# Sparse attention and a feed-forward layer on one core: the third batch's first transposes go ahead of a load, and four units of matmuls move in front of its scores

## The chip, the core and the metric

The kernel runs on one core of a Trainium2 chip. The core has a matrix engine (TensorE, PE in the profile), a vector engine (VectorE, DVE), a scalar engine (ScalarE, ACT) that applies functions and copies, a general engine (GpSimd, POOL) and a queue that gives out transfers (SyncE, SP). All work side by side, and each takes its own instructions in order: what waits at the head of an engine's queue holds whatever stands behind it. The metric is device time of the whole program in microseconds (us), as the median of several executions.

## The reference

Eight batches of eight heads, head size 64. Each head has 512 local and 32 global positions. A local query sees its neighbours up to 32 away and all global keys; a global query sees everything. The outputs of all heads are put side by side and go through a feed-forward layer with a hard-swish.

```python
s_g = scale * q_g @ concat(k_g, k_l).T           # global rows see everything
out_g = softmax(s_g) @ concat(v_g, v_l)
s_ll = where(abs(i - j) <= 32, scale * q_l @ k_l.T, -1e9)
s_l = concat(scale * q_l @ k_g.T, s_ll)
out_l = softmax(s_l) @ concat(v_g, v_l)
x = concat(out_g, out_l) -> (8 * 544, 512)       # heads side by side
h = x @ w_in                                     # 512 -> 2048
g = h * clip(h + 3, 0, 6) / 6
out = g @ w_out                                  # 2048 -> 512
```

## The kernel before

**Attention** works on pairs of heads. A batch has four pairs (NM is 4), so the program has 32 pairs, numbered p = 4 * batch + m. For each pair:

- `load(p)` gives SP the transfers of k, q and v into staging buffers (`stg`, 16 of them, 256 KB each); a transfer can be given only when its buffer is free.
- `cast(p, "kq", nc.gpsimd)` has POOL turn them into 16-bit `kn` and `qn`. `first(p, what)` casts and also copies half of v to other partitions (`vshift`).
- k and q must be transposed. For the first two batches TensorE does this (`emit_T`). From the third batch on (pair 8 = `2 * NM`) `emit_TD(p)` gives SP two DMA transposes, L244 for k into `kT`, L245 for q into `qT`.
- `wrap_q(p)` (L251) has ScalarE copy the last 32 columns of the transposed q to its front. It waits for the q transpose.
- `emit_S2(p)` multiplies the scores (L263, 16 small matmuls into four PSUM buffers), takes their exponentials on ScalarE (L267) and masks them on VectorE (L270). Pair p's scores read what `wrap_q(p)` wrote.
- `emit_SG(p)` does the global queries' scores, `emit_AV(p)` multiplies by v and normalises, `emit_PG(p)` does the global rows' sums, and `emit_X(p)` transposes the result for the feed-forward layer.

**The feed-forward layer** is cut into units that `M(n)` places between the steps of attention, n at a time, from a list. A unit `u1(c)` is four matmuls (L421) into one PSUM buffer, an evicting function on ScalarE (L426, writes `t`) and a product on VectorE (L428, writes `gt`). A unit `u2(t, c4)` is four matmuls (L437) of the second product; every fourth one is copied out and stored (L441, L443). The pool `psp` has seven PSUM buffers, shared by scores, units and transposes. A batch's units come into the list after its attention, so they run beside the next batch.

**The order.** Up to `wrap_q(2 * NM)` and the unit behind it, all five engines' orders are fixed as the program is written, by `pin(*ALL)`. From there on only the transfer queue and POOL are fixed (`pin(*QUEUES)`); the order on TensorE, VectorE and ScalarE is chosen when the program is built, by a scheduler, and it may put a later instruction ahead of the fixed ones where its operands allow.

Around the third batch's start the program is written like this (the parts that the change touches):

```python
    emit_TD(2 * NM)                # transposes of pair 8
    load(2 * NM + 2)               # pair 10
    ...
    emit_TD(2 * NM + 1)            # transposes of pair 9
    ...
    M(4)
    emit_den(1)                    # global rows of batch 1: a matmul,
    emit_XG(1)                     # logarithms (L405), an exponential (L406)
    wrap_q(2 * NM)
    M(1)
    pin(*ALL)
    emit_S2(2 * NM)
```

In the loop that follows, `feed(p)` calls `wrap_q(p + 1)`, casts pair p + 4, gives the transposes of pair p + 3 and the loads of pair p + 5; then come the scores of pair p + 1, the attention of pair p, and units in four groups n[0] to n[3] between them.

Of the kernel before, what the change touches and what calls it, by code (L numbers as in the profile page):

```python
# [14 lines left out]
def kernel(  # L15
# [12 lines left out]
    nc = tc.nc  # L28
# [5 lines left out]
    NM = H // 2  # L34
# [20 lines left out]
    def ps_tile(name, dtype=FP32):  # L55
        return psp.tile([P, 2048 // (4 if dtype == FP32 else 2)], dtype, tag="ps", name=name)
# [54 lines left out]
    def stage():  # L111
        return wrk.tile([P, 512], FP32, tag="stg", name="stg", bufs=NSTG)

    def load(p, what="kqv"):
        b, m = divmod(p, NM)
        s = st.setdefault(p, {})
        for c in what:
            src = {"k": k_l, "q": q_l, "v": v_l}[c]
            t = stage()
            if c != "v" and b < NRUN:  # L120
                nc.sync.dma_start(out=t.rearrange("p (h x) -> p h x", h=2),  # L121
                                  in_=src[b, 2 * m:2 * m + 2].rearrange("h (p j) d -> p h (j d)", j=NT))
            else:
                nc.sync.dma_start(out=t.rearrange("p (h kb d) -> p (h kb) d", h=2, kb=NT),
                                  in_=src[b, 2 * m:2 * m + 2].rearrange("h (kb p) d -> p (h kb) d", p=P))
            s[c + "f"] = t.rearrange("p (h kb d) -> p kb h d", h=2, kb=NT)

    def cast(p, what, eng):
        b, m = divmod(p, NM)
        s = st[p]  # L130
        for c in what:
            if c == "v":
                o = vts[b % NV][:, :, m, vc].rearrange("p kb (h d) -> p kb h d", h=2)
            else:
                s[c + "n"] = wrk.tile([P, NT, P], FP16, tag=c + "n", name=c + "n", bufs=4)
                o = s[c + "n"].rearrange("p kb (h d) -> p kb h d", h=2)
            eng.tensor_copy(out=o, in_=s[c + "f"])  # L137
# [27 lines left out]
    def cast_w(kind, i, eng):  # L165
        if kind == "in":
            qd, m = divmod(i, NM)
            o = w_in_t[m][:, qd * 512:(qd + 1) * 512]
        else:
            o = w_out_t[i // 4][:, i % 4]  # L170
        (eng.copy if eng is nc.scalar else eng.tensor_copy)(out=o, in_=w_st[kind, i])  # L171
# [13 lines left out]
    def cast_G(b0, b1, nm, eng=nc.vector):  # L185
        n = wrk.tile([P, 4 * P], FP16, tag="gn", name=nm + "n", bufs=2)
        nb = b1 - b0
        eng.tensor_copy(out=n[:, 0:nb * P], in_=gst[b0, nm][:, 0:nb * P])
        gst[b0, nm, "n"] = n
# [23 lines left out]
    def emit_T(p, qdve=False):  # L213
        b, m = divmod(p, NM)
        s = st[p]
        kT = kTs[b % 2][:, m]
        kv = kT[:, 0:NT * KW].rearrange("p (u c) -> p u c", u=NT)
        qT = wrk.tile([P, Sl + W], FP16, tag="qT", name="qT", bufs=5)
        ps = {}
        for c in "kq":  # L220
            ps[c] = ps_tile("psT" + c, FP16)[:, 0:Sl]
            for j in range(NT):
                nc.tensor.matmul(out=ps[c][:, j * P:(j + 1) * P], lhsT=s[c + "n"][:, j], rhs=ident,
                                 is_transpose=True)
        qcopy = nc.vector.tensor_copy if qdve else nc.scalar.copy
        nc.vector.tensor_copy(
            out=kv[:, :, 0:P].rearrange("p u (i j) -> p u i j", j=NT),
            in_=ps["k"].rearrange("p (j u i) -> p u i j", j=NT, u=NT))
        qcopy(out=qT[:, W:Sl + W].rearrange("p (i j) -> p i j", j=NT),
              in_=ps["q"].rearrange("p (j i) -> p i j", j=NT))  # L230
        if b == 0:
            nc.vector.tensor_copy(out=qT[:, 0:W], in_=qT[:, Sl:Sl + W])
        else:
            nc.scalar.copy(out=qT[:, 0:W].rearrange("p (i j) -> p i j", j=NT),
                           in_=ps["q"].rearrange("p (j i) -> p i j", j=NT)[:, P - W // NT:P])
        s["qT"], s["kT"] = qT, kT

    def emit_TD(p):
        b, m = divmod(p, NM)
        s = st[p]  # L240
        kT = kTs[b % 2][:, m]
        kv = kT[:, 0:NT * KW].rearrange("p (u c) -> p u c", u=NT)
        qT = wrk.tile([P, Sl + W], FP16, tag="qT", name="qT", bufs=5)
        nc.sync.dma_start_transpose(out=kv[:, :, 0:P], in_=s["kn"].rearrange("p u c -> p (u c)"))  # L244
        nc.sync.dma_start_transpose(out=qT[:, W:Sl + W].rearrange("p (u c) -> p u c", u=NT),  # L245
                                    in_=s["qn"].rearrange("p u c -> p (u c)"))
        s["qT"], s["kT"] = qT, kT

    def wrap_q(p):
        qT = st[p]["qT"]  # L250
        nc.scalar.copy(out=qT[:, 0:W], in_=qT[:, Sl:Sl + W])  # L251
# [130 lines left out]
    def emit_X(p):  # L382
        b, m = divmod(p, NM)
        xn = st[p]["xn"]
        if b > 3 or (b == 3 and m < NM - 1):
            xt = wrk.tile([P, Sl], FP16, tag=f"xt{m}", name=f"xt{m}", bufs=2)
            xts.setdefault(b, []).append(xt)
            nc.sync.dma_start_transpose(out=xt.rearrange("p (w c) -> p w c", w=NT),
                                        in_=xn.rearrange("p w c -> p (w c)"))
            return  # L390
        psX = ps_tile("psX", FP16)
        for w in range(NT):
            nc.tensor.matmul(out=psX[:, w * P:(w + 1) * P], lhsT=xn[:, w], rhs=ident,
                             is_transpose=True)
        xt = wrk.tile([P, Sl], FP16, tag=f"xt{m}", name=f"xt{m}", bufs=2)
        xts.setdefault(b, []).append(xt)
        nc.vector.tensor_copy(out=xt, in_=psX[:, 0:Sl])

    def emit_XG(b):
        pg = pgs[b]  # L400
        Lg = wrk.tile([P, NM, Sg], FP32, tag="Lg", name="Lg", bufs=1)
        Rg = wrk.tile([P, NM, Sg], FP32, tag="Rg", name="Rg", bufs=1)
        for e in range(2):
            r = slice(e * D, (e + 1) * D)
            nc.scalar.activation(out=Lg[r], in_=pg[r, 1, :, e], func=LN)  # L405
        nc.scalar.activation(out=Rg, in_=Lg, func=EXP, scale=-1.0)  # L406
        for e in range(2):
            r = slice(e * D, (e + 1) * D)
            nc.vector.tensor_tensor(out=xg[r, :, b], in0=Rg[r], in1=pg[r, 0, :, e], op=mult)
# [56 lines left out]
    def M(n):  # L466
        for _ in range(n):
            if units:
                units.pop(0)()

    def local_dests(b):
        d = []
        for t in range(NT):
            row = b * S + Sg
            if t == 0:
                d.append([(W, P - W, row), (0, W, row + Sl - W)])
            else:
                d.append([(0, P, row + t * P - W)])
        return d
# [28 lines left out]
    for i in range(8, NC):  # L508
        load_w("out", i)
    load(2 * NM, "v")  # L510
    load(2 * NM + 1)

    wz = const("wz", [P, P])
    nc.vector.memset(wz, 0.0)
# [80 lines left out]
    cast(2 * NM, "kq", nc.gpsimd)  # L595
    for i in range(8, NC):
        cast_w("out", i, nc.gpsimd)
    cast(2 * NM + 1, "kq", nc.gpsimd)
    units += moe_units(lambda mm: xts[0][mm], Sl, local_dests(0), early=True)
    u1 = units.pop(0)  # L600
    emit_T(0)
# [34 lines left out]
        u1(c, range(3, 4))  # L636
    u1(4)
    u1(5)
    emit_T(4)
    cast_G(1, 4, "kg")  # L640
    u1(6)
    emit_T(5)
    emit_G(1, 4, "kg")
    emit_S(4, 0)
# [31 lines left out]
    emit_SG(1)  # L676
    M(1)
    emit_TD(2 * NM)
    load(2 * NM + 2)
    emit_X(7)  # L680
    sum_E(0)
# [68 lines left out]
    M(4)  # L750
    emit_den(1)
    emit_XG(1)
    wrap_q(2 * NM)
    M(1)
    pin(*ALL)
# [5 lines left out]
    for p in range(2 * NM, NPAIR):  # L761
        b, m = divmod(p, NM)
        feed(p)
        if p == 10:
            load_g(4, B, "kg")
            load_g(4, B, "qg")
        if p == 12:
            cast_G(4, B, "kg", nc.gpsimd)
            cast_G(4, B, "qg", nc.gpsimd)
        if p == 14:  # L770
            emit_G(4, B, "kg")
        n = (1, 1, 1, 2) if p == 2 * NM else (1, 2, 2, 2) if b in (3, 4) else (1, 2, 2, 3)
        M(n[0])
        if m == 0 and b > NRUN:
            emit_den(b - 1)
            emit_XG(b - 1)
        if p + 1 < NPAIR:
            emit_S2(p + 1)
        M(n[1])
        if p + 1 < NPAIR:  # L780
            emit_SG(p + 1)
        M(n[2])
        emit_AV(p)
        emit_PG(p)
        M(n[3])
        if p == 14:
            emit_G(4, B, "qg")
        emit_X(p)
        if m == NM - 1:
            units += moe_units(lambda mm, b=b: xts[b][mm], Sl, local_dests(b), last=(b == B - 1))  # L790
        pin(*QUEUES)
# [41 lines left out]
```

## Time and profile before

| what | value |
|---|---|
| median of 7 runs | 330.67 us (328.84 to 331.51) |
| the profiled execution's own time | 330.65 us |
| its span on the core | 328.8 us |
| TensorE busy | 308.1 us (94%) |
| VectorE, ScalarE, POOL busy | 217.6, 200.6, 153.1 us |
| mean granted TensorE clock | 0.99 |
| longest wait of TensorE | 7.46 us, before the scores of pair 8 |

The views are read like this. A row of a timeline is start, duration, engine, source line, operation, tiles out and in, shapes, how many instructions were merged, and in brackets the idle time before it with what ended it. A row of the waits is engine, line and what it waited for, then total us, number, longest. A row of the windows is a stretch with each engine's busy time and instruction count in the order PE, PE weight loads, DVE, ACT, POOL, then the granted clock, the DMA engines' busy share and GB/s. SP's rows show the time in which its queue was occupied with an issue; when a transfer lands is told apart from that.

### The profile page before, as it was taken

How to read it: one execution, taken by the hardware profiler on the slowest of the kernel's cores; microseconds unless marked ns; L12 is line 12 of the kernel's file. 1: busy time of each engine (PE TensorE's matmuls, PEld its weight loads, DVE VectorE, ACT ScalarE, POOL GpSimd, SP SyncE). 2: the span in 40 equal slices, each digit the busy share in tenths (PEclk: the TensorE clock that was granted, in tenths of full speed). 3: DMA queues.
4: the chain of work that ended last, by engine and by line, in shares of the span. 5: the costliest groups of instructions: out<-in, count | busy, mean ns of one | idle time of the engine just before them, and what ended most of it. 6: DMA issues, size and time to landing. Idle time of an engine off the chain costs nothing.

```text
span 328.8 us, 7315 instructions
## 1 busy us (share of the span) xinstructions
PE 308.1 (94%) x2673; PEld 163.1 (50%) x2673; DVE 217.6 (66%) x485; ACT 200.6 (61%) x420; POOL 153.1 (47%) x270
## 2 busy tenths in 40 slices
PE   7898999909899999999999989999999999999995
PEld 5553555505455545554455545554555554448444
DVE  6758687828745499857886679458945882379201
ACT  6768877639434499438855777558845971379100
POOL 4877797686944753685447644743521110000000
PEclk9999999978999999999999999999999999999999
DMA  8999999999889978888789978898833102100131
GB/s 214 255 299 313 249 280 308 186 223 204 147 195 230 207 140 146 180 201 175 145 148 214 201 150 146 200 190 158 149 100 107 33 16 77 68 0 3 32 98 64
DMA packets 140260, 53.05 MB, mean 161 GB/s; under 512 B 127552, under 2 KB 131904, under 8 KB 140224
## 3 DMA queue, kind: packets, MB, share of 16 engines
q1 hardware_dynamic: 138048, 52.32, 70.3%
q0 software_dynamic: 2176, 0.26, 1.3%
q8 instruction: 21, 0.34, 0.5%
q14 instruction: 15, 0.12, 0.1%
HBM read 35.13 MB, written 8.91 MB: 134 GB/s over the span
## 4 chain that ended last, share of the span: by engine, by line
PE 57%; DMA 16%; DVE 7%; ACT 6%; POOL 6%; issue 4%; SPq 3%; POOLq 0%; ACTq 0%
PE po L437 29%; PE psH L421 18%; DMA stg<-in_v_l_dram 4%; DVE gt L428 3%; ACT t L426 3%; DMA stg<-in_moe_w_out_dram 3%; DMA qT<-qn 3%; PE psS L263 2%; DMA stg<-in_moe_w_in_dram 2%; DMA stg<-in_q_l_dram 2%; POOL vt L137 2%; SPq L121 2%; ACT E L267 2%; DMA stg<-in_k_l_dram 1%; DVE E L270 1%
## 5 line engine op out<-in xcount | busy, mean ns | idle before, releaser
L437 PE MATMUL po<-wout,gt 128*128 128x512 f16 x528 | 122.8, 379 | 0.3 <-POOL wout L171 0.3
L421 PE MATMUL psH<-xt,win 128*128 128x512 f16 x512 | 121.1, 381 | 2.0 <-DVE gt L428 1.4
L428 DVE SCALAR_TENSOR_TENSOR gt<-t,psH 128x512 f16<-128x512 f32 (+1 forms) x144 | 90.0, 652 | 41.6 <-ACT t L426 40.7
L426 ACT ACTIVATE t<-psH,half_col 128x512 f32<-128x512 f32 (+1 forms) x144 | 91.1, 671 | 12.4 <-PE psH L421 11.2
L421 PEld LDWEIGHTS <-win 128*128 128x128 f16 x576 | 53.5, 98 | 53.2 <-issue 3.5
L437 PEld LDWEIGHTS <-gt 128*128 128x128 f16 x528 | 48.5, 98 | 52.7 <-DVE kgT L206 0.4
L270 DVE TENSOR_TENSOR E<-E,mk 128x512 f16<-128x512 f16 x96 | 54.1, 605 | 7.6 <-ACT E L267 6.3
L267 ACT ACTIVATE E<-psS 128x512 f16<-128x512 f32 x96 | 49.6, 609 | 8.6 <-PE psS L263 8.5
L137 POOL CAST kn<-stg 128x512 f16<-128x512 f32 x31 | 19.3, 623 | 39.2 <-DMA stg<-in_k_l_dram 35.2
L441 ACT COPY ot<-po 128x512 f32<-128x512 f32 x16 | 9.4, 585 | 42.7 <-PE po L437 39.8
L358 POOL TENSOR_TENSOR s<-Eg 128x128 f32<-128x128 f16 x24 | 10.5, 439 | 43.2 <-ACT Eg L307 42.6
L251 ACT COPY qT<-qT 128x32 f16<-128x32 f16 x24 | 5.2, 216 | 37.5 <-DMA qT<-qn 37.4
L340 DVE TENSOR_TENSOR xn<-pav,rc 128x256 f16<-128x256 f32 x64 | 26.1, 421 | 1.5
L137 POOL CAST vt<-stg 128x512 f16<-128x512 f32 x32 | 21.7, 677 | 8.8 <-DMA stg<-in_v_l_dram 8.2
L137 POOL CAST qn<-stg 128x512 f16<-128x512 f32 x31 | 20.5, 661 | 10.6 <-DMA stg<-in_q_l_dram 10.2
L263 PE MATMUL psS<-qT,kT 64*128 64x128 f16 x384 | 16.6, 221 | 8.9 <-ACT qT L251 7.5
L441 DVE COPY ot<-po 128x512 f32<-128x512 f32 x17 | 11.7, 688 | 19.2 <-PE po L437 19.1
L141 POOL COPY vb<-vt 64x512 f16<-64x512 f16 x32 | 20.7, 646 | 2.1
L263 PEld LDWEIGHTS <-kT 64*128 64x128 f16 x384 | 11.5, 96 | 19.5 <-issue 16.8
L292 ACT ACTIVATE E<-psS 128x512 f16<-128x512 f32 x32 | 17.3, 598 | 4.6 <-PE psS L288 4.2
L332 PE MATMUL pav<-vt,E 128*128 128x65 f16 x256 | 20.0, 194 | 0.0
L335 PE MATMUL pav<-vb,E 128*128 128x65 f16 x256 | 20.0, 195 | 0.0
(93 smaller groups left out, 291.7 us busy)
## 6 DMA issues: line engine op xcount, KB each, us to landing
stg<-in_k_l_dram SPq DMA_DIRECT2D x32, 256.0 KB, 3.5
stg<-in_q_l_dram SPq DMA_DIRECT2D x32, 256.0 KB, 4.1
stg<-in_v_l_dram SPq DMA_DIRECT2D x32, 256.0 KB, 4.6
out_dram<-ot SPq DMA_DIRECT2D x23, 256.0 KB, 3.0
stg<-in_moe_w_in_dram SPq DMA_DIRECT2D x16, 256.0 KB, 5.8
stg<-in_moe_w_out_dram SPq DMA_DIRECT2D x16, 256.0 KB, 4.5
out_dram<-ot SPq DMA_DIRECT2D x8, 192.0 KB, 3.7
out_dram<-ot SPq DMA_DIRECT2D x16, 64.0 KB, 1.9
```

What stands on the lines that cost most here:

```text
L137: eng.tensor_copy(out=o, in_=s[c + "f"])
L141: eng.tensor_copy(out=vbs[b % NV][0:D, :, m, vc], in_=vts[b % NV][D:P, :, m, vc])
L263: nc.tensor.matmul(out=pss[2 * ch + e][:, w * P:(w + 1) * P], lhsT=kT[r, c0:c0 + P], rhs=qT[r, w * P:(w + 1) * P])
L267: nc.scalar.activation(out=E[:, ch, e], in_=pss[2 * ch + e], func=EXP, scale=qk_scale)
L270: nc.vector.tensor_tensor(out=E[:, ch, e], in0=E[:, ch, e], in1=mk[:, ch].rearrange("p w c -> p (w c)"), op=mult)
L332: nc.tensor.matmul(out=o, lhsT=E[:, 0, e, w * P:(w + 1) * P], rhs=vt[:, w, m, c], start=True, stop=False, skip_group_check=True)
L340: nc.vector.tensor_tensor(out=xn[:, 2 * w2:2 * w2 + 2].rearrange("p w (e d) -> p w e d", e=2), in0=po[:, :, 1:1 + P].rearrange("p w (e d) ...
L421: nc.tensor.matmul(out=ps[:, 0:n], lhsT=w_in_t[m][:, c * P:(c + 1) * P], rhs=rhs(m), start=(m == 0), stop=(m == NM - 1), skip_group_check= ...
L426: nc.scalar.activation(out=t1[:, 0:n], in_=ps[:, 0:n], func=RELU, bias=half_col, scale=1.0 / 6.0)
L428: nc.vector.scalar_tensor_tensor(out=gts[c][:, 0:n], in0=t1[:, 0:n], scalar=1.0, in1=ps[:, 0:n], op0=amin, op1=mult)
L437: nc.tensor.matmul(out=po[t][:, 0:dm], lhsT=gts[c][:, t * P:(t + 1) * P], rhs=w_out_t[c // 4][:, c % 4], start=(c == 0), stop=(c == NC - 1))
L441: (nc.scalar.copy if t % 2 else nc.vector.tensor_copy)(out=ot, in_=po[t][:, 0:dm])
```

## The change

Five edits:

1. The loads of pair 9 (`2 * NM + 1`: k, q and v) are given to SP behind the DMA transposes of pair 8 and ahead of the loads of pair 10, instead of ahead of those transposes.
2. The cast of pair 9's k and q on POOL is written at the same new place.
3. Unit 6 of the first batch's `u1` is put in front of `emit_T(4)` instead of behind it.
4. Four more units, `M(4)`, stand in front of `wrap_q(2 * NM)`.
5. In the third batch's four pairs the units per pair are 1, 1, 2, 2. Before, they were 1, 1, 1, 2 for the first pair and 1, 2, 2, 3 for the other three.

```diff
@@ -508,7 +508,6 @@
     load(2 * NM, "v")
-    load(2 * NM + 1)
@@ -595,7 +594,6 @@
         cast_w("out", i, nc.gpsimd)
-    cast(2 * NM + 1, "kq", nc.gpsimd)
@@ -636,9 +634,9 @@
     u1(4)
     u1(5)
+    u1(6)
     emit_T(4)
     cast_G(1, 4, "kg")
-    u1(6)
     emit_T(5)
@@ -676,6 +674,8 @@
     emit_TD(2 * NM)
+    load(2 * NM + 1)
+    cast(2 * NM + 1, "kq", nc.gpsimd)
     load(2 * NM + 2)
@@ -750,6 +750,7 @@
     emit_den(1)
     emit_XG(1)
+    M(4)
     wrap_q(2 * NM)
     M(1)
     pin(*ALL)
@@ -769,7 +770,7 @@
-        n = (1, 1, 1, 2) if p == 2 * NM else (1, 2, 2, 2) if b in (3, 4) else (1, 2, 2, 3)
+        n = (1, 1, 2, 2) if b == 2 else (1, 2, 2, 2) if b in (3, 4) else (1, 2, 2, 3)
```

## The prediction

> **What bounds the kernel now.** I read four views in this order: the waits of TensorE, TensorE's timeline around the longest of them, the timelines of the three queues that lead up to it (ACT, SP, POOL), and the table of windows for the clock. TensorE is busy for 308.1 of 328.8 us, so a change can win only idle time and clock. Of the idle 20.7 us, one wait is more than a third:
>
> ```profile
> PE psS L263 <- ACT qT L251: 7.5, 1, 7.5
> ...
> 65.15 1.03 PE L421 MATMUL psH<-xt,win 128*128 128x512 f16 x4
> 73.64 1.04 PE L263 MATMUL psS<-qT,kT 64*128 64x128 f16 x16 [7.46 <-ACT qT L251]
> 74.61 2.85 PE L421 MATMUL psH<-xt,win 128*128 128x512 f16 x8
> ```
>
> The scores of pair 8 (the third batch's first) wait for a copy by ScalarE. What ScalarE did:
>
> ```profile
> 62.65 0.69 ACT L426 ACTIVATE t<-psH,half_col 128x512 f32<-128x512 f32 x1 [0.55 <-PE psH L421]
> 70.75 0.22 ACT L251 COPY qT<-qT 128x32 f16<-128x32 f16 x1 [7.41 <-DMA qT<-qn]
> 70.88 1.84 ACT L426 ACTIVATE t<-psH,half_col 128x512 f32<-128x512 f32 x3
> 72.59 0.55 ACT L405 ACTIVATE Lg<-pg 64x128 f32<-64x128 f32 x2
> 73.17 0.31 ACT L406 ACTIVATE Rg<-Lg 128x128 f32<-128x128 f32 x1
> 73.39 0.20 ACT L251 COPY qT<-qT 128x32 f16<-128x32 f16 x1
> ```
>
> Two copies of L251. The one at 73.39 releases the scores at 73.64, so it is pair 8's. The one at 70.75 waits for a transpose issued at 68.02, which lands 2.7 us later at 70.73; that is pair 9's. Pair 9's copy is written after the fixed part of the program, yet stands in ScalarE's order ahead of three evictions, the two logarithms and pair 8's copy, and everything behind it is held. So the wait is the lateness of pair 9's transposes, seen through ScalarE's queue. They are late because of SP and POOL:
>
> ```profile
> 55.22 0.38 SPq L124 DMA_DIRECT2D stg<-in_v_l_dram  x1
> 55.69 0.53 SPq L124 DMA_DIRECT2D stg<-in_k_l_dram  x1
> 56.32 2.64 SPq L124 DMA_DIRECT2D stg<-in_q_l_dram  x1
> 59.05 0.89 SPq L124 DMA_DIRECT2D stg<-in_v_l_dram  x1
> 60.04 1.95 SPq L244 DMA_TRANSPOSE kT<-kn  x1
> 62.08 2.08 SPq L245 DMA_TRANSPOSE qT<-qn  x1
> 64.21 0.57 SPq L124 DMA_DIRECT2D stg<-in_k_l_dram  x1
> ...
> 66.25 1.65 SPq L244 DMA_TRANSPOSE kT<-kn  x1
> 68.02 1.20 SPq L245 DMA_TRANSPOSE qT<-qn  x1
> ...
> 59.26 0.61 POOL L171 CAST wout<-stg 128x512 f16<-128x512 f32 x1 [0.16 <-DMA stg<-in_moe_w_out_dram]
> 61.74 0.61 POOL L137 CAST kn<-stg 128x512 f16<-128x512 f32 x1 [1.87 <-PE pg L374]
> 62.93 0.61 POOL L137 CAST qn<-stg 128x512 f16<-128x512 f32 x1 [0.57 <-DMA stg<-in_q_l_dram]
> ```
>
> SP gave pair 9's loads at 55.69 to 59.94; the second stood 2.64 us where 0.57 is usual, because its buffer came free only with POOL's weight casts. Pair 8's transposes, whose operands had been cast by 53.5, waited behind them until 60.04. Then the clock:
>
> ```profile
> 65.00:70.00 5.00, 1.18 (x6) 0.48 (x5) 0.27 (x1) 0.00 (x0) 4.62 (x8) 0.97 1.13 207
> 70.00:75.00 5.00, 1.36 (x17) 0.90 (x17) 3.11 (x7) 4.18 (x11) 3.72 (x8) 0.50 1.10 228
> 75.00:80.00 5.00, 5.00 (x38) 2.29 (x37) 3.83 (x8) 4.44 (x10) 2.30 (x6) 0.84 1.01 199
> ```
>
> After the span the last three columns are granted clock, DMA share and GB/s. The shares 0.97, 0.50 and 0.84 are half clock from 69.7 to 76.6; TensorE works from 73.64, so 2.95 us run at half speed and 1.48 us are lost. The stall is worth 7.46 + 1.48 = 8.9 us.
>
> **Part 1, unit 6 ahead of pair 4's transposes.** One unit of four matmuls (0.86 us) changes places with eight transposes (0.45). Its vector product, 0.67 us, now stands ahead of DVE's copy of kT and its cast of kgn, for which TensorE already waits 1.12 us at 29.6; against that, it covers part of the wait for pair 5's casts (0.35), and a wait of 0.47 at 33.4 takes up some slip. Between -0.3 and +0.7 us; I take 0.
>
> **Part 2, the queues.** SP's order becomes v of 8, pair 8's two transposes, pair 9's three loads, pair 10's three loads, pair 9's transposes. On SP nothing is added. Transposes from 55.7, at 1.2 to 2.0 us each, end near 58.4; pair 9's loads leave at 58.5, 59.1 and 60.0 (the last when the final weight cast ends at 59.87). Pair 10's loads follow to 62.5. POOL's order is unchanged: nothing stands between the two places of the cast. Here a rule weighs against the change. The Trainium skill, "DMA: Bandwidth & Descriptors", section "Rules for kernel authors", says to issue a DMA early and wait late; this issues a load 2.8 us later. By the rule alone everything behind pair 9's k shifts by 2.8 us and its last transpose lands at 73.5. By the rows it does not: k took 5.9 us from issue to landing with eight loads on the way and 3.3 to 3.4 in the calmer rows at 64 to 76, so it lands near 62.3 (61.6 now); q could not leave before 58.9 anyway and lands near 63.3 (62.8 now). I take the rows: casts end at 64.0 instead of 63.5. POOL's later work shifts by 0.5, which nobody feels: v of 8, cast by 67.4, is read after 76. Pair 9's transposes then meet a free SP: 62.9 and 64.2, the second landing 2.7 to 3.6 us on, at 67.3 instead of 70.73. Bounds: 66.5 and 73.5.
>
> **Part 3, four more units ahead of the copy.** They add no work to TensorE's total; they are taken from pairs 8 to 11, which give up five (29 to 24; the fifth goes behind). What they add is four evictions of 0.61 (1.84 / 3) on ScalarE ahead of pair 8's copy, 2.45 us. Where pair 9's copy will stand I can't see, since its place isn't fixed by the program; nearest is where it stands now, after the first eviction. Then, from its landing at 67.3: the 2.91 us that now lie between 70.73 and 73.64, plus 2.45, so the scores start at 72.7. TensorE has 3.45 us of new units to 68.6; seven PSUM buffers hold exactly three old and four new outputs, the last unit needs one back (67.3 + copy 0.15 + eviction 0.61 + product 0.65 = 68.75), and ends at 69.6. Idle: 0.15 + 3.1 = 3.2 us instead of 7.46. That wins 4.2.
>
> The clock: the trace's drop came 3.6 us after TensorE fell idle. The Trainium skill, "TensorE: Matmul & The Clock Gate", section "What's actually happening", puts it at a free-running window of about 3.4 us found idle. A gap of 3.1 keeps full clock under both; were it 3.5, the row would still save 1.48 us and the page only if the window fell badly. I count 1.48. Sum so far 5.7.
>
> **Part 4, six units a pair.** Pair 8 goes from 1,1,1,2 to 1,1,2,2, pairs 9 to 11 from 1,2,2,3. Pair 8's two waits for its normalised values (0.66 and 0.26) should shrink; pairs 9 to 11 lose one unit of cover ahead of attention and one behind. From the rows at 86.5 to 92.3: masks end 3.8 us after the scores, a copy of 0.68 and 1.15 for normalising make 5.7; the output transposes are due at 5.6. So 0 to 0.4 a pair. The period falls from 8.6 to 6.9 us while the DMA engines are 0.95, 0.82 and 0.94 busy in the windows of 10 us from 80 to 110; transposes land 13 us ahead of the scores now (81.9 against 95.08), so TensorE is covered, but ScalarE meets its copies earlier (waits of 0.72, 1.61 and 2.02 us at 90 to 109) and can hold an eviction. I charge 0.7 for all of this, bounds -0.6 and +4. If that cover went, pairs would run at the DMA's pace, 0.90 x 8.6 = 7.7 us instead of 6.9, so 0.8 a pair.
>
> Sum: 5.7 - 0.7 = 5.0 us. The profiled run took 330.65 us (span 328.8 and 1.85 around it), beside the median 330.67: 325.6 us.
>
> **Rivals.** *ScalarE's copy of pair 9 lands behind the new evictions.* Then nothing is held, the scores start at 69.5, and nearly all of 8.9 is won: 322. For it: its load is issued later; against: its casts hardly move. *The gain is given back.* Six units a pair make DMA the bound for 27 us: 0.90 busy x 8.6 / 6.9 = 1.12, a backlog of 3.3 us, which reaches TensorE through ScalarE's held evictions, the last of them up to 1 us more: 329 to 330. Against: 13 us of slack. *Slower: the new evictions lengthen the held queue.* If pair 9's transposes land no earlier, scores start 5.36 us after landing instead of 2.91. It decides at 71.7: later than that (1 us later than now) the four units no longer pay for the queue. At the rule's 73.5 the scores start at 78.9, 1.8 us worse than 73.64 + 3.45, with the clock lost as before: 332.5, and more with part 4. For it: pair 9's loads do move behind two transposes that took four us; against: SP's own 2 us of standing.
>
> **How the numbers follow.** Likeliest case 0.42 (325.6, 323.5 to 327.5), copy behind the evictions 0.20 (322), given back 0.14 (329.5), slower 0.24 (332.5). A difference of 0.3%, about 1 us, is what a measurement of this kernel can tell from none. Faster: 0.41 + 0.20 + 0.05 = 0.66; within: 0.08; slower: 0.26. The range 321.5 to 332.5 leaves out half of the slower case and the best of the second.
>
> **What would show it.** Right: SP row L244 near 55.7; a transpose landing near 67.3; TensorE's wait for L251 near 3 us with full granted clock in 70 to 80; pairs 8 to 12 about 6.9 us apart. Wrong: pair 9's cast starting after 65, ScalarE's wait before L251 longer than 6, a second wait for L251 between 80 and 110, or idle TensorE before L393 of over 0.5 us a pair.

## The result and the profile after

The changed kernel takes 328.43 us (median of 27 runs, 325.36 to 331.68) where the kernel before, beside it, took 331.09 (median of 64). The ratio is 0.9924, interval 0.9906 to 0.9942: 2.5 us faster. (Here and below a ratio is estimated from runs in the faster of the kernel's two states, with a 95% interval, and need not be exactly the quotient of the two medians.) The forecast was 325.6, so the direction holds and the size is half of what was forecast. The profiled execution took 327.49 us, with a span of 325.7.

The waits of TensorE after (engine, line, what it waited for; total us, number, longest):

```profile
PE psS L263 <- ACT qT L251: 2.7, 1, 2.7
PE psH L421 <- DVE gt L428: 2.7, 5, 1.6
```

The wait of 7.46 us before the scores of pair 8 has become two. TensorE's timeline from the four units ahead of `emit_den(1)` to the scores of pair 9:

```profile
63.43 3.62 PE L421 MATMUL psH<-xt,win 128*128 128x512 f16 x16
66.89 0.27 PE L379 MATMUL pg<-Es,ones 128*128 128x256 f16 x1
67.00 3.62 PE L421 MATMUL psH<-xt,win 128*128 128x512 f16 x16
72.23 1.02 PE L421 MATMUL psH<-xt,win 128*128 128x512 f16 x4 [1.61 <-DVE gt L428]
75.99 1.04 PE L263 MATMUL psS<-qT,kT 64*128 64x128 f16 x16 [2.74 <-ACT qT L251]
76.96 3.06 PE L437 MATMUL po<-wout,gt 128*128 128x512 f16 x8
81.83 0.62 PE L263 MATMUL psS<-qT,kT 64*128 64x128 f16 x16
```

Four units run from 67.00, a fifth waits 1.61 us for a PSUM buffer, and the scores wait 2.74 us for pair 8's copy. Idle together: 4.35 us. ScalarE in the same stretch:

```profile
64.50 0.69 ACT L426 ACTIVATE t<-psH,half_col 128x512 f32<-128x512 f32 x1 [0.53 <-PE psH L421]
70.65 0.22 ACT L251 COPY qT<-qT 128x32 f16<-128x32 f16 x1 [5.47 <-DMA qT<-qn]
70.78 1.84 ACT L426 ACTIVATE t<-psH,half_col 128x512 f32<-128x512 f32 x3
72.50 0.55 ACT L405 ACTIVATE Lg<-pg 64x128 f32<-64x128 f32 x2
73.08 0.31 ACT L406 ACTIVATE Rg<-Lg 128x128 f32<-128x128 f32 x1
73.41 2.42 ACT L426 ACTIVATE t<-psH,half_col 128x512 f32<-128x512 f32 x4
75.70 0.23 ACT L251 COPY qT<-qT 128x32 f16<-128x32 f16 x1
```

Pair 9's copy (70.65) still stands at the same place in ScalarE's order, behind one eviction, and holds the queue for 5.47 us. Behind it now come three evictions, the logarithms and the four new evictions, and only then pair 8's copy (75.70). SP tells why pair 9's transpose landed at 70.65:

```profile
55.52 1.62 SPq L244 DMA_TRANSPOSE kT<-kn  x1
57.24 2.09 SPq L245 DMA_TRANSPOSE qT<-qn  x1
59.38 0.57 SPq L124 DMA_DIRECT2D stg<-in_k_l_dram  x1
...
61.59 0.94 SPq L124 DMA_DIRECT2D stg<-in_k_l_dram  x1
62.58 1.13 SPq L124 DMA_DIRECT2D stg<-in_q_l_dram  x1
63.75 1.14 SPq L124 DMA_DIRECT2D stg<-in_v_l_dram  x1
65.01 3.06 SPq L244 DMA_TRANSPOSE kT<-kn  x1
68.17 1.21 SPq L245 DMA_TRANSPOSE qT<-qn  x1
```

The rows at 55.52 and 57.24 are pair 8's transposes, 4.5 and 4.8 us earlier than before: SP has done what the change says. But pair 10's three loads (61.59 to 64.89) keep pair 9's transposes until 65.01. The clock, in two views of windows (granted clock, DMA share and GB/s are the last three columns):

```profile
30.00:35.00 5.00, 4.21 (x21) 1.67 (x22) 2.61 (x8) 2.13 (x5) 4.29 (x8) 0.66 1.00 243
...
70.00:75.00 5.00, 1.64 (x7) 0.57 (x6) 3.32 (x7) 4.28 (x10) 4.71 (x10) 1.00 1.02 216
75.00:80.00 5.00, 4.01 (x29) 1.97 (x29) 3.30 (x7) 3.52 (x9) 1.18 (x2) 0.66 1.22 203
...
69.10:72.50 3.40, 1.78 (x10) 0.73 (x8) 1.01 (x2) 1.85 (x5) 3.20 (x6) 1.00 0.80 172
72.50:75.90 3.40, 0.75 (x4) 0.23 (x3) 3.21 (x7) 3.33 (x9) 3.18 (x6) 1.00 1.28 222
75.90:79.30 3.40, 3.31 (x22) 1.64 (x22) 1.76 (x5) 1.93 (x6) 0.34 (x1) 0.51 1.13 216
```

The clock is full while TensorE waits and half from 75.9 to 79.3, just when it works again: the scores take 1.04 us instead of 0.62, the next eight matmuls 3.06 instead of 1.90, which is 1.58 us lost.

A table by stage shows where the 3.14 us between the two profiles' last matmuls (325.31 and 322.17) lie. Units that one kernel does in a stage and the other elsewhere are counted at 0.86 us each.

| stage | before | after | after, with before's units | difference |
|---|---|---|---|---|
| start to `emit_den(1)` | 65.04 | 66.89 | 66.89 | +1.85 |
| to the scores of pair 9 | 14.23 | 14.94 | 11.49 | -2.74 |
| to the scores of pair 12 | 24.38 | 20.53 | 23.12 | -1.26 |
| to the scores of pair 16 | 32.63 | 31.20 | 32.92 | +0.29 |
| to the end | 189.03 | 188.61 | 187.75 | -1.28 |

I don't put the first row down to the change. Up to 1.7 us of it is another stretch of half clock, from 31.6 to 35.0, where TensorE was busy throughout (granted clock 0.66 from 30 to 35; 1.00 before). The kernel before with only ScalarE's order changed (e12 below) has such a stretch too, and over the other profiles below (e10 left out, which stalls ahead of it) `emit_den(1)` starts anywhere from 64.69 to 68.52, in kernels with and without the edits.

Nor can the first two rows be read apart, since the stall ends a fixed time after pair 9's landing, whenever TensorE arrives. In e6 and e7 below, the changed kernel with one edit taken back and with two copies on POOL moved, `emit_den(1)` starts at 65.76 and 65.09, earlier than the 66.89 here, and yet pair 9's scores start at 82.28 and 81.99, as late as the 81.83 here. So the two rows belong together: up to pair 9's scores, four units taken off, the change won 0.89 us.

Other profiles tell which rows last. Three have the old units per pair (before, e3, e5) and three the new ones (this one, e6, e7). The third row holds in all six: 24.38 to 24.41 us against 20.53. The last does not: with before's units it is 189.03, 187.85 and 187.89 us against 187.75, 188.33 and 188.13. On the means of three the change won 0.76 us up to pair 9's scores, 1.27 to those of pair 12, lost 0.24 to those of pair 16 and won 0.19 behind them: 2.0 us in all, where the medians say 2.5.

### The profile page after: what moved, and what is told of

It reads as the page before. It is cut to its first block, busy times and chain, and to the rows that moved or that the text cites. A ratio compares the mean times of both kernels' runs of the same rounds, so it can differ in the third digit from the quotient of the medians.

```text
span 325.7 us, 7320 instructions
## 1 busy us (share of the span) xinstructions
PE 309.8 (95%) x2673; PEld 163.6 (50%) x2673; DVE 214.5 (66%) x485; ACT 199.6 (61%) x420; POOL 151.6 (47%) x270
## 4 chain that ended last, share of the span: by engine, by line
PE 68%; DMA 13%; DVE 7%; POOL 3%; ACT 3%; SPq 3%; issue 1%; POOLq 0%; ACTq 0%
PE po L437 32%; PE psH L421 23%; DVE gt L428 5%; DMA stg<-in_v_l_dram 3%; PE psS L263 3%; DMA stg<-in_q_l_dram 3%; DMA stg<-in_moe_w_in_dram 2%; ACT t L426 2%; DMA qT<-qn 2%; DMA stg<-in_k_l_dram 2%; PE pav L332 2%; DMA stg<-in_moe_w_out_dram 2%; PE pav L335 2%; SPq L121 2%; PE po L449 1%
## 5 line engine op out<-in xcount | busy, mean ns | idle before, releaser
L428 DVE SCALAR_TENSOR_TENSOR gt<-t,psH 128x512 f16<-128x512 f32 (+1 forms) x144 | 90.1, 652 | 31.6 <-ACT t L426 30.4
L270 DVE TENSOR_TENSOR E<-E,mk 128x512 f16<-128x512 f16 x96 | 52.4, 584 | 30.7 <-ACT E L267 29.5
L137 POOL CAST qn<-stg 128x512 f16<-128x512 f32 x31 | 19.8, 639 | 11.6 <-DMA stg<-in_q_l_dram 11.4
L137 POOL CAST vt<-stg 128x512 f16<-128x512 f32 x32 | 20.9, 654 | 7.2 <-DMA stg<-in_v_l_dram 5.9
L332 PEld LDWEIGHTS <-E 128*128 128x128 f16 x256 | 17.8, 99 | 3.4
```

The source lines that it names most:

```text
L270: nc.vector.tensor_tensor(out=E[:, ch, e], in0=E[:, ch, e], in1=mk[:, ch].rearrange("p w c -> p (w c)"), op=mult)
L332: nc.tensor.matmul(out=o, lhsT=E[:, 0, e, w * P:(w + 1) * P], rhs=vt[:, w, m, c], start=True, stop=False, skip_group_check=True)
L428: nc.vector.scalar_tensor_tensor(out=gts[c][:, 0:n], in0=t1[:, 0:n], scalar=1.0, in1=ps[:, 0:n], op0=amin, op1=mult)
```

## The experiments

**The theory**: one copy, standing by the scheduler's choice at the head of ScalarE's queue for data that come late, sets the stall; the change only shortens the hold. **Rivals**: the stall is pair 8's or the DMA engines' own lateness, or the gain comes from the queue order or from the units alone.

**e1 and e2: take the copy's freedom away.** Until pair 12, ScalarE keeps the written order, in the kernel before (e1) and in the changed one (e2).

```diff
-        pin(*QUEUES)
+        pin(*QUEUES, *((ET.Activation,) if p < 3 * NM else ()))
```

> The kernel before, with ScalarE's order fixed as written through the third batch, so that pair 9's copy cannot stand ahead of the evictions; nothing else moves. Theory (the stall of 7.46 us is pair 9's copy at the head of ScalarE's queue): pair 8's own transpose landed at 65.7, so its scores start at about 66.5 instead of 73.64, pair 9's wait for its own copy at about 71 instead of 79.27, and the kernel is 6 to 9 us faster, near 323 to 325. Rival (pair 8's data are late whatever the order): scores still near 73, time within 1 us of before.

> The changed kernel with the same fixed order on ScalarE. Theory: the two waits left (1.61 and 2.74 us) and the half clock after them (about 1.7 us) go, pair 8's scores start near 71.4 instead of 75.99, and it is 4 to 6 us faster than the changed kernel, near 323. Rival (the transposes hold TensorE anyway): the wait moves to the scores of pair 9 and less than 2 us is won.

e1: 325.23 us, ratio 0.9812 (0.9766 to 0.9859). e2: 323.65 us, 0.9789 (0.9743 to 0.9836). TensorE's timeline and ScalarE's in e1, with none of the change's edits:

```profile
67.74 0.27 PE L379 MATMUL pg<-Es,ones 128*128 128x256 f16 x1
67.85 1.03 PE L421 MATMUL psH<-xt,win 128*128 128x512 f16 x4
69.56 0.62 PE L263 MATMUL psS<-qT,kT 64*128 64x128 f16 x16 [0.69 <-ACT qT L251]
...
69.31 0.20 ACT L251 COPY qT<-qT 128x32 f16<-128x32 f16 x1
```

Pair 8's copy runs at 69.31, without waiting for anything, and the stall is 0.69 us instead of 7.46. That is the held queue, shown; pair 8's own data were there by then. In e2 the scores follow the last unit with 0.02 us between. The full granted clock holds in both. In both, one wait is left before the scores of pair 12 (1.52 us each). ScalarE in e2 tells why:

```profile
96.74 0.22 ACT L251 COPY qT<-qT 128x32 f16<-128x32 f16 x1 [4.43 <-DMA qT<-qn]
96.98 0.59 ACT L441 COPY ot<-po 128x512 f32<-128x512 f32 x1
97.46 0.22 ACT L251 COPY qT<-qT 128x32 f16<-128x32 f16 x1
```

The fixed order ends just there, and two copies stand together again, the first waiting 4.43 us for its transpose. e9 tests whether the first is pair 13's, put ahead of pair 12's.

**e3, e4, e5: the change's parts, each alone in the kernel before.** e3 is the two queue edits, e4 the four units and six per pair, e5 unit 6.

```diff
-    load(2 * NM + 1)
...
     emit_TD(2 * NM)
+    load(2 * NM + 1)
+    cast(2 * NM + 1, "kq", nc.gpsimd)
...
+    M(4)
     wrap_q(2 * NM)
...
-        n = (1, 1, 1, 2) if p == 2 * NM else (1, 2, 2, 2) if b in (3, 4) else (1, 2, 2, 3)
+        n = (1, 1, 2, 2) if b == 2 else (1, 2, 2, 2) if b in (3, 4) else (1, 2, 2, 3)
...
+    u1(6)
     emit_T(4)
     cast_G(1, 4, "kg")
-    u1(6)
```

> The kernel before with the queue edits alone (pair 9's loads and cast behind pair 8's transposes). Theory: pair 9's transpose lands at 70.6 to 70.8 as in both kernels, since SP and POOL only change the order of the same waits; no difference over 1 us, 330 to 331.5. Rival (the prediction's step: it lands at 67.3): 3 us faster, near 327.5.

> The kernel before with the four more units ahead of the copy and six units a pair, and neither the queue edits nor unit 6's move. Theory: the units fill 3.45 us of the stall and cost 2.45 us of evictions ahead of the copy, so idle before pair 8's scores falls from 7.46 to about 4.5 to 6.5 and with the better first pair it is 1.5 to 3.5 us faster, 327.5 to 329.5. Rival (the longer held queue eats them): within 1 us of before.

> The kernel before with unit 6 of the first product in front of the pair-4 transposes, and nothing else. If the early loss of 1.85 us in the changed kernel's profile (its stage reaches the same unit at 63.43 instead of 61.59) is this edit's, the profile shows waits for pair 5's casts of about 1.4 us and a half-clock stretch near 32, and the same 1.2 to 2 us more at the first unit ahead of pair 8; the stall behind it swallows part of that, so 0 to 1 us slower. If it was that execution's transfers, no early loss and within 0.5 us of before.

e3: 331.18 us, 1.0029 (1.0006 to 1.0052). e4: 329.39 us, 0.9962 (0.9941 to 0.9983). e5: 330.91 us, 0.9986 (0.996 to 1.0012). ScalarE's first row is e3's, TensorE's three are e4's:

```profile
69.87 0.22 ACT L251 COPY qT<-qT 128x32 f16<-128x32 f16 x1 [6.88 <-DMA qT<-qn]
```

```profile
66.03 3.62 PE L421 MATMUL psH<-xt,win 128*128 128x512 f16 x16
73.27 1.87 PE L421 MATMUL psH<-xt,win 128*128 128x512 f16 x4 [3.62 <-DVE gt L428]
77.02 1.04 PE L263 MATMUL psS<-qT,kT 64*128 64x128 f16 x16 [1.89 <-ACT qT L251]
```

With the queue edits alone the copy's data land at 69.87, and nothing is won: the stall is still 6.93 us. With the units alone pair 8's scores start later, at 77.02 instead of 73.64, as four more evictions stand ahead of its copy; but TensorE does 3.45 us of work meanwhile, its idle time is 5.51 us in two pieces instead of 7.46, and 1.3 us are won. e5's profile has half clock from 30.0 to 33.4 and comes to the units ahead of `emit_den(1)` at 63.49 instead of 61.59, two of the three signs of the first case of its expectation (the waits for pair 5's casts are only 0.6 us), and yet its time is that of before. As e12 has such a stretch without unit 6's move and e7 has none with it, the stretch is not put down to the move. The three parts add to a ratio near 0.998, the whole has 0.9924, which points to queue edits and units that help each other; how they do it is not shown.

**e6: the change without unit 6's move.**

```diff
     u1(5)
-    u1(6)
     emit_T(4)
     cast_G(1, 4, "kg")
+    u1(6)
```

> The changed kernel with unit 6 back behind the pair-4 transposes: queue edits and units together. The sum of the two alone is -0.1% (+0.3 and -0.4). If unit 6's move costs time, this is faster than the changed kernel, near 327. If the edits only add up, it is near 330 and unit 6's move is worth 2 us; if queue edits and units help each other, it is near 328.4 like the changed kernel.

328.66 us, 0.9924 (0.989 to 0.9957), the same ratio as with it. Unit 6 is worth nothing that can be measured, in either kernel.

**e7: is it POOL that makes pair 9 late?** The two copies of the global keys and values go behind pair 9's transposes.

```diff
-    vglob(2, nc.gpsimd)
-    kglob(2, nc.gpsimd)
...
     emit_TD(2 * NM + 1)
+    vglob(2, nc.gpsimd)
+    kglob(2, nc.gpsimd)
     load(2 * NM + 3)
```

> The changed kernel with POOL's two copies of the third batch's global keys and values (L144, L210) behind pair 9's transposes instead of ahead of v's casts. Theory: the k transpose of pair 9, given at 65.01 and held to 68.07, waits for POOL's copy into the same tile, which ends at 67.45; without it the transposes land near 68.7 instead of 70.65, everything on ScalarE moves 1.9 us forward, the scores of pair 8 start near 74 and it is 1.5 to 3 us faster than the changed kernel, near 326. Rival (SP's backlog of transfers holds it): it still lands at 70 or later, within 0.7 us of the changed kernel.

328.76 us, 0.9919 (0.9891 to 0.9948): no gain on the changed kernel. SP in e7:

```profile
61.02 0.90 SPq L124 DMA_DIRECT2D stg<-in_k_l_dram  x1
61.96 2.40 SPq L124 DMA_DIRECT2D stg<-in_q_l_dram  x1
64.41 1.24 SPq L124 DMA_DIRECT2D stg<-in_v_l_dram  x1
65.76 1.54 SPq L244 DMA_TRANSPOSE kT<-kn  x1
67.40 1.20 SPq L245 DMA_TRANSPOSE qT<-qn  x1
```

That theory fell. The first transpose does hold SP for only 1.54 us, but so it does in e6 (1.66), where POOL's copies stand as in the changed kernel. And SP comes to pair 9's transposes no earlier with POOL relieved, because pair 10's loads stand ahead of them on SP itself and take 4.54 us here.

**e8: e2 without unit 6's move.** Beside e2's edit:

```diff
-    u1(6)
     emit_T(4)
     cast_G(1, 4, "kg")
+    u1(6)
```

> The changed kernel with ScalarE's order fixed through the third batch and unit 6 back at its place. With no stall left behind it, what unit 6's move does at 26 to 33 us should reach the end: against the same kernel with the move (323.65) it is 0 to 1.5 us faster if the move costs, 0.5 slower if it fills a wait.

324.83 us, 0.9814 (0.9766 to 0.9861), its interval over e2's: unit 6 is worth nothing measurable where no stall could swallow it either.

**e10: pair 9's transposes ahead of pair 10's loads.** The direct test of what e7 pointed to.

```diff
     load(2 * NM + 1)
     cast(2 * NM + 1, "kq", nc.gpsimd)
+    emit_TD(2 * NM + 1)
     load(2 * NM + 2)
...
     first(2 * NM + 1, "v")
-    emit_TD(2 * NM + 1)
```

> The changed kernel with pair 9's two transposes given to SP directly behind pair 9's loads and ahead of pair 10's loads. Theory (pair 10's three issues, 0.9 to 1.1 us each, are what keeps SP until 65.0 and makes the prediction's landing at 67.3 a miss): the first transpose is issued near 63.7, the second near 65.0 right behind its cast, landing near 67.7 instead of 70.65; ScalarE's wait for it falls from 5.5 to about 2.5 us, TensorE's two waits before pair 8's scores from 4.35 to 1.5 or less, and the time by 2 to 3 us against the changed kernel: ratio to before about 0.985. Rival (the loads of pair 9 themselves land late, or the DMA engines are full, so that the landing stays at 69.5 or later whatever stands in SP's queue): ratio 0.992, stall above 3.5 us. Second rival (pair 10's loads, held behind transposes that wait for a cast, come late): landing early, but a wait of TensorE or ScalarE for pair 10 between 80 and 95, ratio 0.990 or above.

329.2 us, 0.9947 (0.9921 to 0.9972). SP, ScalarE, VectorE and TensorE in e10:

```profile
63.84 1.28 SPq L244 DMA_TRANSPOSE kT<-kn  x1
65.24 1.20 SPq L245 DMA_TRANSPOSE qT<-qn  x1
```

```profile
67.71 0.22 ACT L251 COPY qT<-qT 128x32 f16<-128x32 f16 x1 [6.55 <-DMA qT<-qn]
67.96 3.00 ACT L426 ACTIVATE t<-psH,half_col 128x512 f32<-128x512 f32 x5
```

```profile
68.68 0.69 DVE L428 SCALAR_TENSOR_TENSOR gt<-t,psH 128x512 f16<-128x512 f32 x1 [6.86 <-ACT t L426]
...
71.84 0.37 PE L379 MATMUL pg<-Es,ones 128*128 128x256 f16 x1 [6.04 <-DVE Es L352]
78.39 0.62 PE L263 MATMUL psS<-qT,kT 64*128 64x128 f16 x16
```

Half of the theory holds to the tenth: the transpose lands at 67.7, and no load of pair 10 is missed. The time does not follow. The scheduler now puts pair 9's copy further forward, ahead of ten evictions instead of seven, so ScalarE starts to wait at 61.2 instead of 65.2 and waits longer, 6.55 us. VectorE starves behind it and TensorE stops for 6.04 us at `emit_den(1)`, before the four units that were to cover a stall. The stall has moved to an earlier place where nothing covers it. None of the three cases written down for e10 names this.

**e9, e11, e12: ScalarE's order fixed through all pairs**, in the changed kernel (e9), in e10's (e11) and in the kernel before (e12).

```diff
-        pin(*QUEUES)
+        pin(*QUEUES, ET.Activation)
```

> The changed kernel with ScalarE's order kept as written through all pairs, not just to pair 11 as in e2. Theory (the same mechanism works wherever the scheduler may put a later pair's copy first): e2's wait of 1.52 us before the scores of pair 12, behind pair 13's copy, goes away, and the 2.1 us idle in the fourth batch fall below 1; 1.5 to 3 us faster than e2, ratio to the kernel before about 0.972. Rival (the scheduler's order is better than the written one once the pipeline runs, or pair 12 simply waits for its own data): no gain on e2 or a loss, ratio 0.979 or above, with new small waits of TensorE for L251 or for evictions after 100.

> e9 and e10 together. Theory (with ScalarE's order as written nothing waits behind pair 9's copy, so an earlier landing is worth nothing): as e9, ratio about 0.972, within 0.3% of it. Rival (the landing counts by itself, or the copies of later pairs profit): over 0.3% faster than e9; or slower than e9 by over 0.3% because pair 10's loads come late.

> The kernel before with ScalarE's order kept as written through all pairs, and nothing else. It tells what the change is worth once no copy can stand ahead of others. Theory (the change's gain was relief of the held queue, and its five edits are worth little by themselves; e1 against e2 gave 0.2% between them): ratio to the kernel before 0.966 to 0.970, within 0.4% of e9, no wait of TensorE for L251 above 0.5 us. Rival (six units a pair and the queue order are worth something of their own, the 2.2 us by which the changed kernel runs pairs 8 to 12 with shorter waits): 0.6% or more slower than e9, ratio 0.973 or above, with waits before attention between 70 and 105.

e9: 319.32 us, 0.9665 (0.9624 to 0.9707). e11: 320.77 us, 0.9699 (0.9658 to 0.9739). e12: 319.41 us, 0.9649 (0.9607 to 0.9691). The intervals of the three lie over each other, and e9's lies below e2's. TensorE's waits of over 0.1 us between 95 and 260 us in e2, then in e12:

```profile
PE psH L421 <- DVE gt L428: 1.8, 5, 0.6
PE psS L263 <- DMA stg<-in_k_l_dram: 1.5, 1, 1.5
PE psS L263 <- DVE gt L428: 1.1, 3, 0.4
PE psH L421 <- ACT E L267: 0.2, 1, 0.2
```

```profile
PE psS L263 <- ACT qT L251: 0.2, 1, 0.2
```

Of 4.6 us of waits in the later pairs 0.2 is left. The wait of 1.52 us before pair 12 was the same thing one batch on, with the load that the trace names only the last of several that the wait hangs on. The smaller waits behind it, put down to VectorE, went with the same line; that each of them was a copy out of place is not shown. e9 came out better than the 0.972 expected. e11 equals e9 within the intervals, so an earlier landing is worth nothing that can be measured once nothing stands behind it. e12 answers what the change is worth by itself: with the order fixed, the kernel before runs as fast as the changed one, within the intervals of about 0.4%. e9 and e12 beat both kernels: e12 took 319.41 us beside 331.72 for the kernel before, 12.3 us less, and by the ratios (0.9649 against 0.9924) some 9 us less than the changed kernel. It does so with one line.

## Why the prediction was right or wrong

**The bound: right.** The stall before pair 8's scores is pair 9's copy at the head of ScalarE's queue. e1 takes that away, and the idle time there falls from 7.46 to 0.69 us (with 0.83 more before pair 9).

**Part 1: right.** Taken as 0; e5, e6 and e8 each find nothing measurable. They could not tell less than about 1 us from nothing, so the reasons given for it are not tested.

**Part 2, the landing at 67.3: this step failed.** The last transpose landed at 70.65, against 70.73 before. The step "pair 9's transposes then meet a free SP: 62.9 and 64.2" is the false line. Three terms were too small. Pair 8's transposes ended at 59.33, not 58.4: the two were sized at 2.7 us, though the same two rows of before, 1.95 and 2.08, make 4. Pair 10's issues took until 64.89, not 62.5: they were sized at the short durations of calm rows and took 0.94, 1.13 and 1.14 us. And pair 9's first transpose occupied SP for 3.06 us instead of 1.2 to 2.0. This is no accident of one execution: from pair 9's first load to the end of its second transpose SP needs 9.6 to 10.0 us for the eight issues (pair 9's and pair 10's loads and the two transposes) in all seven profiles with this order (the changed kernel, e2, e3, e6, e7, e8, e9), where the prediction had about 6.9 (58.5 to 64.2, and 1.2 for the last, the lower of its two rates). The casts were nearly right: predicted to end at 64.0, they ended at 64.8. The rule of the Trainium skill that was weighed there ("DMA: Bandwidth & Descriptors", "Rules for kernel authors": issue early, wait late) would have put the landing at 73.5. 70.65 lies halfway between the two; what came late was the issue of the transposes, not the load's data. e10 shows the order on SP that gives 67.7.

**Part 3, the length of the held queue: right to 0.02 us.** It was put at 2.91 plus 2.45, so 5.36 us from landing to scores; it measured 75.99 less 70.65, 5.34. The copy stayed where it was taken to stay. The same stretch is 5.33 us in e4 and 5.34 in e6 and e7. As the landing was late, idle time fell by 3.11 us and not by 4.2. TensorE itself also reached this point 1.85 us later in the profiled execution, which hid part of the miss: landing came 3.8 us after `emit_den(1)` started, where 2.3 was predicted. In e6 and e7, where it reached the point earlier, idle time fell only to 5.43 and 5.37 us.

**Part 3, the clock: this step failed.** "A gap of 3.1 keeps full clock" did not hold. The gaps were only 1.61 and 2.74 us, with a unit between them, and still half clock followed, costing 1.58 us where none was predicted. The Trainium skill's section "What's actually happening" of "TensorE: Matmul & The Clock Gate" speaks of an idle window of about 3.4 us. The window from 72.5 to 75.9 in the windows shown above was not idle: it had 0.75 us of work, 22%. In the same view the window ahead of it, 69.1 to 72.5, had 1.78 us of work, and full clock followed. So here a window mostly idle was enough. It is no clean share of work: the earlier stretch of half clock follows 3.4 us with 1.56 us of work (46%), and the one in e12 follows 1.89 us (55%). In e6 and e7, too, half clock comes, for 6.8 us from 73.1 and 73.7. The fault was to compare the longest single gap with the window, and not to add up what work falls into one.

**Part 4: wrong in sign.** The charge was 0.7 us. From pair 9's scores to pair 12's the new split came out 1.26 us better, and all six profiles named above show this stage alike. No wait for normalised values is left there, where before had 0.92. The period of pairs 9 to 12 was 6.84 us, against 6.9 predicted, and no DMA backlog reached TensorE. Up to pair 16's scores some 0.2 us were lost, and behind them nothing certain was won: idle time after pair 16 is 2.27 us before and 1.12 after, but e3 and e5, with the old split, have 1.30 and 1.62. e12, with the old split and a fixed order, takes 23.12 us from pair 9 to pair 12, as much as the changed kernel with three units added (23.12), so six units a pair are not needed for this gain: ScalarE's order alone does it.

The sum: up to pair 9's scores 5.7 us were forecast and 0.89 won. The two failed steps make up the difference: the landing came 3.35 us later than forecast, and half clock cost 1.58 us, which leaves 0.8. The later pairs, from pair 9's scores on, gave 2.25 us in the two profiles, and 1.2 on the means of three, instead of costing 0.7. That the miss is not larger is luck: Part 4's error has the other sign.

**The rivals.** "The copy lands behind the evictions, 322" is what e1 and e2 make by hand, and their full gain (323.65 for e2) is about the size named. "The new evictions lengthen the held queue" was real, 5.34 us from landing to scores, but its landing of 71.7 was not reached. e4 tests its arithmetic: the landing stands there where it stood before (5.8 us after `emit_den(1)` starts, against 5.7), so the four units should bring 3.45 us less 2.45 of longer queue, 1.0; it was 1.3 us faster. "The gain is given back" named 329 to 330, near the measured 328.43, but for another reason: the DMA backlog it rests on did not come.

What stays open: why one issue stands so long on SP. In each of the seven profiles one of these eight does, but not the same one: pair 9's first transpose in the changed kernel (3.06 us), its second in e9 (2.22), a load of pair 10 in the others (2.16 to 2.48). POOL's copy into the same tile, e7's theory, does not explain the first transpose: in e9 it has left SP by 66.69, before that copy starts at 66.80.

## What to carry to other kernels

When an engine waits long for a small instruction, look at what stands behind it in that engine's order, and whether the program or a scheduler put it there: fixing the order was worth 3.5%, the whole change 0.8%. Where the order is free, an edit that brings an operand forward can move its reader forward too, so that the wait starts earlier and costs as much (e10). And when one such wait is removed, look for the same pattern at each later place where the freedom begins again: here the first stall's removal gave 1.9 to 2.1%, and 1.2 to 1.6% more lay in the later pairs.

## What was not expected of the hardware

Half clock lasted for about 3.4 us or a multiple of it in every profile, wherever it fell ahead of the program's last 10 us: 3.4 us twice in the changed kernel, 6.8 around the stalls of before, e3, e5, e6, e7 and e10, 10.2 in e4. It falls late: in the changed kernel it fell as work began again, so the matmuls behind the gap pay for it.

An issue of the same load on SP took 0.57 us in calm stretches and 0.9 to 2.5 us for pair 10's loads (61 to 68 us) where they follow pair 9's. How busy the DMA engines are does not tell which: the share from 60 to 65 us is 1.26 in the changed kernel, but 1.36 before, where pair 10's first two loads took 0.57 each at 64.21 and 64.84. A plan of SP's time made from the calm rows was 2.4 us short from pair 8's first transpose to pair 10's last load.
